# Other tiles for normalisation, cluster products, one-hot turns and odd heads' one-hot transfers in a fused attention and mixture kernel

## The chip, the core and the metric

One core of a Trainium2 chip runs the whole program; nothing is spread over several cores. The metric is the time of one execution in microseconds (us), the median of several runs. The engines are PE (TensorE matmuls, PEld its weight loads), DVE (VectorE), ACT (ScalarE), POOL (GpSimd) and SP, whose queue issues the DMAs. Each engine works through its instructions in the order in which the program wrote them, and waits on semaphores for what others make.

## What is computed

Attention in which a query sees only the keys of its own cluster, then two feed-forward layers, all in float32:

```python
q_assign = np.argmax(np.einsum('bhsd,hcd->bhsc', q_n, c_n), axis=-1)
k_assign = np.argmax(np.einsum('bhsd,hcd->bhsc', k_n, c_n), axis=-1)
mask = q_assign[:, :, :, None] == k_assign[:, :, None, :]
scores = np.where(mask, scale * np.matmul(q, k.transpose(0, 1, 3, 2)), -1000000000.0)
attn = softmax(scores)                       # 2 x 8 heads, 768 tokens, 64 wide, 16 clusters
x = np.matmul(attn, v)                       # -> 1536 x 512
x = np.maximum(x @ w_in, 0.0) ** 2 @ w_out   # 512 -> 2048 -> 512
out = sum_e p[:, e] * (np.maximum(x @ w1[e], 0.0) @ w2[e])   # 4 experts, 512 -> 1024 -> 512
```

## The kernel before, in words

Float32 products are made of three (or two) products of rounded halves, a high and a low part of each operand. The change touches only the attention stage, the first 331 us; the layers behind it are the same program.

**Tiles and rounds.** The 16 heads have six query tiles of 128 rows each, so the loop over `g` has 96 tiles. I count them in rounds of twelve: round r holds the tiles of heads 2r and 2r+1 (tile 0 to tile 11 of the round), and tile n of round r is g = 12r + n. In tile g PE makes the scores of tile g+2 (`emit_S`, L572), transposes the exponentials of tile g (L605) and makes half of the product with V of an earlier pair of tiles (L619, L621). DVE takes the row maximum (L581) and the low halves (L611); ACT the exponential (L592) and the high halves (L610). The order of these pieces within a tile is the written list `ORDER`, one for even and one for odd tiles. A score tile has a second product, of one-hot cluster rows (in `k2` and `q2`), which lifts the matching keys.

**Work for the pair of heads to come.** During round r the one-hots of pair r+1 (heads 2r+2 and 2r+3) are made, at tiles given by the table `AT` as offsets from that pair's first tile. Each such step takes one of two places (`X1`, `X2`) in a tile on PE, and its evacuation stands at `Y1` or `Y2`. All of them use one PSUM tile, `m`. The steps:
- four transposing steps (`trans_slot`, L354) in tiles 10 and 11 of the round before; ACT copies, then POOL splits into `nkh`, `nkl`, `nqh`, `nql` (L52 and L363).
- `pair_scores` twice (L404): the products with the cluster centres, four matmuls for half the tokens, which read the split keys and queries; ACT copies to `ys`.
- `pair_turn` twice (L420): three transposes each, summed by DVE into `A` (L425). The second one appends the steps of `pair_ops` to the list `dq`.
- `pair_ops`: a maximum on DVE (L456, called m1 below), three operations on POOL that mark the first winner (L446 to L448, p1), a second maximum on DVE (L457, m2), and four operations on POOL that write the one-hots `oh` (L451 to L454, p2). Even tiles take two entries of `dq`, odd tiles three, at the letters `C`. Between p1 and m2 stand `AT["gap"]` empty entries. Pair 1 makes p2's part on DVE (`last`, L463 to L466).
- `pair_hot` (L478): empties `dq`, transposes `oh` on PE (three transposes), ACT copies to `ohm` (L483), and SP writes the even head's one-hot rows by four DMAs (`hot_rows`, L495). The odd head's four DMAs are issued at the offset `ohd`.

**Normalisation of the pair before.** `norm_slots(r-1)` enters `nq` at the end of tile 1 of round r, and one entry is taken per tile from tile 2 on: f1 puts four small DVE operations (L661 to L664) in front of `dq`, f2 transposes them (L670) and lets POOL add two halves of the output (`xs`, two operations, L679), and f3 twice (L687) spreads the factors; POOL then multiplies, rounds and takes the low part (L694, L52, L707).

**Also on these engines.** `split_v` (POOL, L52 and L295) at tiles 3 and 9. In rounds 1 to 4 one step of the weight conversion `convert` (letter `K`) stands at the end of every even tile: DVE operations of 128x512, such as L171 and L176, and once a round one on ACT and POOL (L182, L184). The SP queue also carries the stacked copies of `nkh`, `nql` and so on (`stack`, L375, L377).

Of the kernel before, what the change touches and what calls it, by code (L numbers as in the profile page):

```python
# [12 lines left out]
ALU = mybir.AluOpType  # L13
AX = mybir.AxisListType
# [10 lines left out]
    "S T0 X1 M E T1 R Y1 X2 H0 P0 C H1 L0 L1 C K Y2".split(),  # L25
    "S X1 E M T0 T1 Y1 H0 C P1 X2 R L0 H1 C L1 O Y2 C".split()]
WARM = [12, 10, 5, 11, 3, 9]
START = {'t': [0, 1, 1, 2], 'a': [3, 4, 4, 5, 8], 'stack1': 4, 'stack': 5, 'head': [0, 2]}
AT = {"gap": 3, "stack1": -11, "stack": -9, "oh": -4, "ohd": -4, "splitv": -3, "load": -8,
      "t": [-14, -14, -13, -13], "a": [-11, -11, -10, -10, -4], "conv": 8}  # L30


@with_exitstack
def moe_attention_kernel(
# [15 lines left out]
    def round_pool(dst, src):  # L50

        nc.gpsimd.tensor_scalar(dst, src, 1.0, 1.0, op0=ALU.mult, op1=ALU.mult)  # L52
# [28 lines left out]
    wgt = const.tile([128, 1, C], F32, name="wgt")  # L81
# [117 lines left out]
    with tc.manual_schedule():  # L199
# [235 lines left out]
        def pair_ops(j, A):  # L435
            mx = as_p.tile([128, 4 * NTT, 1], F32, tag="mx", name="mx")
            mx2 = as_p.tile([128, 4 * NTT, 1], F32, tag="mx2", name="mx2")
            off = as_p.tile([128, NTT, 2, C], F32, tag="off", name="off")
            oh = ohs["p", j] = as_p.tile([128, NTT, 2, 2, C], F32R, tag="oh", name="oh")
            shp = [128, 4 * NTT, C]  # L440
            V, P = nc.vector, nc.gpsimd
            av = A.rearrange("p (t x e) c -> p t x e c", x=2, e=2)
            mv = mx2.rearrange("p (t x e) c -> p t x e c", x=2, e=2)

            def p1():
                P.tensor_tensor(A, A, mx.to_broadcast(shp), op=ALU.subtract)  # L446
                P.tensor_scalar(A, A, 2.0 ** 63, 2.0 ** 63, op0=ALU.mult, op1=ALU.mult)
                P.tensor_tensor(A, A, wgt.to_broadcast(shp), op=ALU.add)  # L448

            def p2():  # L450
                P.tensor_tensor(A, A, mx2.to_broadcast(shp), op=ALU.subtract)  # L451
                P.tensor_scalar(oh[:, :, :, 0], av[:, :, 1], 0.0, -1.0, op0=ALU.min, op1=ALU.max)
                P.tensor_scalar(off, av[:, :, 0], 0.0, -1.0, op0=ALU.min, op1=ALU.max)
                P.tensor_scalar(oh[:, :, :, 1], off, 1.0, -NEG, op0=ALU.add, op1=ALU.mult)  # L454

            head = [lambda: V.reduce_max(out=mx, in_=A, axis=AX.X), p1]  # L456
            m2 = lambda: V.reduce_max(out=mx2, in_=A, axis=AX.X)  # L457
            if j > 1:
                return head + [lambda: None] * AT["gap"] + [m2, p2]

            def last(e):
                w = [128, NTT, C]
                V.tensor_tensor(off[:, :, e], av[:, :, 0, e], mv[:, :, 0, e].to_broadcast(w),  # L463
                                op=ALU.not_equal)
                V.tensor_scalar(oh[:, :, e, 1], off[:, :, e], NEG, None, op0=ALU.mult)
                V.tensor_tensor(oh[:, :, e, 0], av[:, :, 1, e], mv[:, :, 1, e].to_broadcast(w),  # L466
                                op=ALU.is_equal)
            return head + [lambda: None] * 3 + [m2, lambda: last(0), lambda: last(1)]

        def pair_hot(j):  # L470

# [87 lines left out]
        def pair_slots(j):  # L559
            return [trans_slot(j, nm, half) for nm in ("nk", "nq") for half in range(2)]  # L560
# [92 lines left out]
        def norm_slots(hp, last=False):  # L653
            st = {}
            def f1():
                sm = sums_t.pop(hp)
                r = sm_p.tile([128, 2, NTT], F32, tag="r", name="r", bufs=1)
                rs = st["rs"] = sm_p.tile([128, NTT, 2, 2], F32R, tag="rs", name="rs", bufs=2)
                rv = r.rearrange("p h t -> p t h")
                dq[:0] = [  # L660
                    lambda: nc.vector.tensor_scalar(r, sm, 1e-9, None, op0=ALU.add),  # L661
                    lambda: nc.vector.reciprocal(r, r),
                    lambda: nc.vector.tensor_copy(rs[:, :, :, 0], rv),
                    lambda: nc.vector.tensor_tensor(  # L664
                        rs[:, :, :, 1], rv, rs[:, :, :, 0].bitcast(F32), op=ALU.subtract),
                ]

            def f2():
                m = ps_m.tile([NTT * 4, 128], F32R, tag="m", name="m")
                nc.tensor.transpose(m, st["rs"].rearrange("p t h s -> p (t h s)"), identr)  # L670

                def evac():
                    rt = st["rt"] = xs_p.tile([NTT * 4, 128], F32R, tag="rt", name="rt")
                    nc.scalar.copy(rt, m.bitcast(F32))
                    if hp in xm_t:
                        xm = xm_t.pop(hp)
                        for c0 in range(0, S, HALF):
                            cs = slice(c0, c0 + HALF)
                            nc.gpsimd.tensor_tensor(  # L679
                                xs_t[hp][:, cs], xs_t[hp][:, cs], xm[:, cs], op=ALU.add)  # L680
                return evac

            def f3(half):
                b, kt = divmod(hp, H // 2)
                m = ps_m.tile([128, HALF], F32, tag="m", name="m")
                for j in range(QT):
                    nc.tensor.matmul(  # L687
                        m[:, j * 128:(j + 1) * 128], sel[:, half * QT + j], st["rt"],
                        start=True, stop=True)

                def evac():
                    rb = xs_p.tile([128, HALF], F32, tag="rb", name="rb")
                    nc.scalar.copy(rb, m)
                    (nc.vector if last else nc.gpsimd).tensor_tensor(  # L694
                        rb, rb, xs_t[hp][:, half * HALF:(half + 1) * HALF], op=ALU.mult)
                    c0 = b * S + half * HALF
                    col = c0
                    while col < c0 + HALF:
                        tb, o = divmod(col, TB)
                        n = min(TB - o, c0 + HALF - col)  # L700
                        xn = rb[:, col - c0:col - c0 + n]
                        hi = xh[tb][:, kt, o:o + n]
                        if last:
                            nc.scalar.copy(hi, xn)
                        else:
                            round_pool(hi, xn)
                        (nc.vector if last else nc.gpsimd).tensor_tensor(  # L707
                            xl[tb][:, kt, o:o + n], xn, hi.bitcast(F32), op=ALU.subtract)
                        col += n
                return evac  # L710

            return [f1, None, None, f2, lambda: f3(0), lambda: f3(1)]


        mp = {}
# [320 lines left out]
        def at(d, g, f):  # L1036
            d.setdefault(max(g, 0), []).append(f)

        for i in range(1, NH):
            u0 = i * NTT  # L1040
            if i > 1:
                for n, x in enumerate(("stack1", "stack")):
                    at(early, START[x] if i == 2 else u0 + AT[x], lambda i=i, n=n: stack(i, n))
                if i % 2:
                    at(early, u0 + AT["ohd"], lambda i=i: hot_rows(i))
            else:
                for n in range(2):
                    at(slots, START["head"][n], onehot_slot(i) if n else assign_slot(i))
            at(early, u0 + AT["splitv"], lambda i=i: split_v(i))
            if i + 1 < NH:  # L1050
                at(early, u0 + AT["splitv"] + 1, lambda i=i: load_v(i + 1))
        for j in range(1, NH // 2):
            u0 = 2 * j * NTT
            for n, f in enumerate(pair_slots(j)):
                at(slots, START["t"][n] if j == 1 else u0 + AT["t"][n], f)
            for n, f in enumerate([pair_scores(j, 0), pair_scores(j, 1), pair_turn(j, 0),
                                   pair_turn(j, 1), pair_hot(j)]):
                at(slots, START["a"][n] if j == 1 else u0 + AT["a"][n], f)
            if j + 1 < NH // 2:
# [88 lines left out]
            gemm1(*its[n], ps=s[:, 0])  # L1148

        hp, pr = NH // 2 - 1, NU // 2 - 1  # L1150
        f1, _, _, f2, f3, f4 = norm_slots(hp, last=True)
        f1()
        while dq:
            dq.pop(0)()
# [44 lines left out]
        def r_ops(b, ops):  # L1199
# [8 lines left out]
        head = {  # L1208
            -1: [("t", RT3), ("t", RT1), ("h", RT1), ("t", RT2), ("l", RT1)],
            0: [("h", RT2), ("h", RT3), ("t", RT4), ("l", RT2)],  # L1210
            1: [("l", RT3), ("h", RT4), ("h", RB22)],
            2: [("l", RT4), ("l", RB22)]}
# [89 lines left out]
```

## Time and profile before

| | |
|---|---|
| median of 3 runs | 1083.51 us (1083.09 to 1084.83) |
| profiled execution | 1086.17 us, of which the span of the trace is 1083.2 us |
| busy in the span | PE 1035.2 us, DVE 682.3, ACT 537.3, POOL 561.3 |
| from 0 to 330.8 us (attention) | PE 286.8 us, DVE 241.9, ACT 236.1, POOL 163.2 |
| from 330.8 us to the end | PE 748.4 us of 752.4 |

The page gives busy time for each engine; an engine can be idle between instructions for want of data, and rows of the trace show for such a gap its length and what ended it. Behind 330.8 us PE is busy for all but 4 us. In the attention stage it is not busy for 44 us. The median lies 2.66 us under the profiled execution's own time, which has 2.97 us around its span.

### The profile page before, as it was taken

The numbers are of one execution on the slowest core, as the hardware profiler recorded it, in microseconds if no ns is written. First come the engines' busy times: TensorE is split into PE (matmuls) and PEld (weight loads), VectorE is DVE, ScalarE is ACT, GpSimd is POOL, SyncE is SP. The second block draws the span as 40 slices with busy tenths as digits, with TensorE's granted clock in tenths as the row PEclk, the third lists the DMA queues.
The fourth block names the chain that finished last, engine by engine and source line by source line (L and its number), as shares of the span: only waits on it lengthen the run. The fifth ranks groups of instructions, "written<-read, shape, count | busy, mean of one in ns | idle before, by whom it ended". The sixth has DMA issues, their size and how long they took to land.

```text
span 1083.2 us, 14977 instructions
## 1 busy us (share of the span) xinstructions
PE 1035.2 (96%) x5558; PEld 915.9 (85%) x5558; DVE 682.3 (63%) x1072; ACT 537.3 (50%) x1080; POOL 561.3 (52%) x546
## 2 busy tenths in 40 slices
PE   8897889889799999999999999999999999999998
PEld 7787778779788888888888988889898899888897
DVE  8786677567767777373126655657767555555554
ACT  6686677668775554344434333433445333334331
POOL 4365564564322222223445666667668766666650
PEclk9998998899999999999999999999999999999999
DMA  4663554556202233021101221122123212211201
GB/s 114 158 142 81 128 121 100 125 139 162 67 1 78 85 110 99 19 96 60 39 1 40 78 78 61 57 78 78 45 73 131 83 40 79 78 66 52 78 1 58
DMA packets 72408, 86.05 MB, mean 79 GB/s; under 512 B 26896, under 2 KB 49744, under 8 KB 72336
## 3 DMA queue, kind: packets, MB, share of 16 engines
q1 hardware_dynamic: 72336, 85.11, 27.4%
q8 instruction: 43, 0.70, 0.3%
q14 instruction: 29, 0.24, 0.1%
HBM read 59.83 MB, written 3.15 MB: 58 GB/s over the span
## 4 chain that ended last, share of the span: by engine, by line
PE 85%; DVE 6%; POOL 5%; ACT 1%; issue 1%; SPq 1%; DMA 1%; POOLq 0%; ACTq 0%; DVEq 0%
PE bank L893 24%; PE bank L853 21%; PE bank L746 12%; PE s L572 4%; PE bank L727 4%; PE bank L729 4%; PE bank L728 4%; PE t L605 3%; PE po L619 2%; PE po L621 2%; DVE nb L581 2%; DVE ptl L611 1%; POOL xa L707 1%; POOL rb L694 1%; PE m L404 1%
## 5 line engine op out<-in xcount | busy, mean ns | idle before, releaser
L893 PE MATMUL bank<-w1h,ga 128*128 128x512 f32 x768 | 269.9, 393 | 0.0
L903 DVE SCALAR_TENSOR_TENSOR x<-bank,pe_p,x 128x512 f32<-128x512 f32 x180 | 134.9, 751 | 167.8 <-PE bank L893 167.8
L853 PE MATMUL bank<-xa,w0h 128*128 128x384 f32 x896 | 228.3, 335 | 0.1
L853 PEld LDWEIGHTS bank<-xa,w0h 128*128 128x128 f32 x896 | 164.5, 188 | 17.9 <-ACT fa L864 0.5
L893 PEld LDWEIGHTS bank<-w1h,ga 128*128 128x128 f32 x768 | 144.1, 188 | 24.5
L736 POOL TENSOR_TENSOR ga<-fa,ga 128x512 fp32r<-128x512 f32 x48 | 62.3, 1299 | 182.0 <-ACT ga L735 139.5
L893 PE MATMUL bank<-w1l,ga 128*128 128x512 f32 x384 | 151.6, 395 | 0.0
L853 PE MATMUL bank<-xa,w0l 128*128 128x384 f32 x448 | 149.7, 334 | 0.0
L611 DVE TENSOR_TENSOR ptl<-t,pth 128x384 fp32r<-128x384 f32 x192 | 98.2, 548 | 52.5 <-ACT pth L610 52.0
L864 ACT COPY fa<-bank 128x384 f32<-128x384 f32 x96 | 45.5, 474 | 171.7 <-PE bank L853 171.7
L746 PE MATMUL bank<-ga,w1h 128*128 128x512 f32 x384 | 126.7, 389 | 0.0
L873 ACT ACTIVATE ga<-fa 128x384 fp32r<-128x384 f32 x96 | 50.5, 527 | 135.6 <-DVE fa L867 135.6
L822 POOL TENSOR_TENSOR w0l<-raw,w0h 128x512 fp32r<-128x512 f32 x64 | 75.0, 1195 | 81.4 <-ACT w0h L821 81.4
L840 POOL TENSOR_TENSOR w1l<-raw,w1h 128x1024 fp32r<-128x1024 f32 x32 | 77.2, 2414 | 71.3 <-ACT w1h L839 71.3
L581 DVE TENSOR_REDUCE nb<-s 128x1 f32<-128x768 f32 x96 | 91.5, 953 | 26.5 <-PE s L572 25.7
L610 ACT CAST pth<-t 128x384 fp32r<-128x384 f32 x192 | 84.1, 488 | 23.7 <-PE t L605 23.2
L572 PE MATMUL s<-k,q 80*128 80x384 f32 (+1 forms) x384 | 88.8, 353 | 3.3 <-DMA k<-ohm 3.1
L605 PE MATMUL t<-identf,p 128*128 128x128 f32 x576 | 89.9, 283 | 1.6 <-DVE ptl L611 1.5
L876 DVE SCALAR_TENSOR_TENSOR ga<-fa,ga 128x384 fp32r<-128x384 f32 x96 | 90.1, 938 | 0.6 <-ACT ga L873 0.6
L592 ACT ACTIVATE p<-s,nb 128x768 f32<-128x768 f32 x96 | 87.4, 910 | 2.4 <-DVE nb L581 1.9
L733 ACT ACTIVATE fa<-bank 128x512 f32<-128x512 f32 x44 | 26.3, 598 | 118.1 <-PE bank L729 116.7
L746 PEld LDWEIGHTS bank<-ga,w1h 128*128 128x128 f32 x384 | 72.0, 188 | 14.7
(202 smaller groups left out, 2086.0 us busy)
## 6 DMA issues: line engine op xcount, KB each, us to landing
raw<-in_moe_w_dram SPq DMA_DIRECT2D x64, 512.0 KB, 4.1
raw<-in_moe_w_in_dram SPq DMA_DIRECT2D x8, 1024.0 KB, 5.2
raw<-in_moe_w_out_dram SPq DMA_DIRECT2D x6, 1024.0 KB, 4.9
k<-nkh SPq DMA_DIRECT2D x28, 192.0 KB, 3.3
q<-nqh SPq DMA_DIRECT2D x28, 192.0 KB, 3.0
nv<-in_v_dram SPq DMA_DIRECT2D x16, 192.0 KB, 3.8
out_dram<-x SPq DMA_DIRECT2D x12, 256.0 KB, 2.1
k<-nkl SPq DMA_DIRECT2D x14, 192.0 KB, 3.7
```

The lines of the kernel that those rows point to most:

```text
L572: nc.tensor.matmul(s[:, j, 0:HALF], stk[i, nq][:, t * 128:(t + 1) * 128], stk[i, nk][:, j * HALF:(j + 1) * HALF], start=first, stop=not first)
L581: nc.vector.tensor_reduce(out=nb, in_=s_ps[u][:, :, 0:HALF], axis=AX.XY, op=ALU.max, negate=True)
L592: nc.scalar.activation(p, s_ps.pop(u)[:, :, 0:HALF], AF.Exp, bias=nb_t.pop(u), accum_out=sums_t[hp][:, i % 2, t:t + 1])
L605: nc.tensor.transpose(tp[:, j], p_sb[u][:, half, j * 128:(j + 1) * 128], identf)
L610: return (lambda: nc.scalar.copy(dh, tp), lambda: nc.vector.tensor_tensor(dl, tp, dh.bitcast(F32), op=ALU.subtract))
L611: lambda: nc.vector.tensor_tensor(dl, tp, dh.bitcast(F32), op=ALU.subtract))
L746: nc.tensor.matmul(o, a, b, start=(ft == 0 and z == 0), stop=(ft == NF - 1 and z == 2))
L840: nc.gpsimd.tensor_tensor(lo, w, hi.bitcast(F32), op=ALU.subtract)
L853: nc.tensor.matmul(ps, w[:, o:o + 128], r_op(r, x)[:, kt], start=(first and kt == 0 and z == 0), stop=(kt == 1 and z == 2), skip_group_che ...
L876: nc.vector.scalar_tensor_tensor(out=g_t(n, f, t, 1), in0=h_src(n, f, t), scalar=0.0, in1=g_t(n, f, t, 0).bitcast(F32), op0=ALU.max, op1=A ...
L893: nc.tensor.matmul(o, a, w[:, f], start=(f == 0 and z == 0), stop=(f == 1 and z == 2))
L903: nc.vector.scalar_tensor_tensor(out=acc, in0=o, scalar=pc, in1=acc, op0=ALU.mult, op1=ALU.add)
```

## The change

Numbers in two tables and two lists of steps move.
- `pair_scores` goes from tile 1 (both) to tiles 0 and 1, `pair_turn` from tile 2 (both) to tiles 1 and 2, and `pair_hot` from tile 8 to tile 7. For pair 1, which has its own table `START`, only `pair_hot` moves, from tile 8 to tile 7 of round 0.
- The gap between p1 and m2 is two empty entries, not three.
- The odd head's `hot_rows` go from tile 2 of its own round to tile 11 of the round before (`ohd` from -4 to -7).
- Normalisation: two empty entries come between f2 and f3, so both f3 stand in tiles 8 and 9, not 6 and 7. The last pair's, behind the loop, is the same work.
- Pair 1 marks the first winner on DVE (two operations) and not on POOL (three), with no empty entries.

```diff
-START = {'t': [0, 1, 1, 2], 'a': [3, 4, 4, 5, 8], 'stack1': 4, 'stack': 5, 'head': [0, 2]}
-AT = {"gap": 3, "stack1": -11, "stack": -9, "oh": -4, "ohd": -4, "splitv": -3, "load": -8,
-      "t": [-14, -14, -13, -13], "a": [-11, -11, -10, -10, -4], "conv": 8}
+START = {'t': [0, 1, 1, 2], 'a': [3, 4, 4, 5, 7], 'stack1': 4, 'stack': 5, 'head': [0, 2]}
+AT = {"gap": 2, "stack1": -11, "stack": -9, "ohd": -7, "splitv": -3, "load": -8,
+      "t": [-14, -14, -13, -13], "a": [-12, -11, -11, -10, -5], "conv": 8}
...
-            return head + [lambda: None] * 3 + [m2, lambda: last(0), lambda: last(1)]
+            return [m1, lambda: V.tensor_tensor(A, A, mx.to_broadcast(shp), op=ALU.is_equal),
+                    lambda: V.tensor_tensor(A, A, wgt.to_broadcast(shp), op=ALU.mult),
+                    m2, lambda: last(0), lambda: last(1)]
...
-            return [f1, None, None, f2, lambda: f3(0), lambda: f3(1)]
+            if last:
+                return [f1, f2, lambda: f3(0), lambda: f3(1)]
+            return [f1, None, None, f2, None, None, lambda: f3(0), lambda: f3(1)]
```

**POOL, from `split_v` of tile 3 to p2, in the round that prepares pair 6.** Before, the two additions L679 come first, then p1, and then both f3 (L694 begins each):

```order
L679 TENSOR_TENSOR xs<-xs,xm 128x384 x2
L446 TENSOR_TENSOR A<-A,mx 128x384
L447 TENSOR_SCALAR A<-A 128x384
L448 TENSOR_TENSOR A<-A,wgt 128x384
L694 TENSOR_TENSOR rb<-rb,xs 128x384
```

Five rows further, in the same program, the second f3 and behind it p2 (L451 to L454):

```order
L694 TENSOR_TENSOR rb<-rb,xs 128x384
L52 TENSOR_SCALAR xa<-rb 128x384
L707 TENSOR_TENSOR xa<-rb,xa 128x384
L451 TENSOR_TENSOR A<-A,mx_3122 128x384
L452 TENSOR_SCALAR oh<-A 128x12x16
L453 TENSOR_SCALAR off<-A 128x192
L454 TENSOR_SCALAR oh<-off 128x12x16
```

After the change (two lines further down in the file, so L679 is L681 and L694 is L696):

```order
L446 TENSOR_TENSOR A<-A,mx 128x384
L447 TENSOR_SCALAR A<-A 128x384
L448 TENSOR_TENSOR A<-A,wgt 128x384
L681 TENSOR_TENSOR xs<-xs,xm 128x384 x2
L451 TENSOR_TENSOR A<-A,mx_3110 128x384
L452 TENSOR_SCALAR oh<-A 128x12x16
L453 TENSOR_SCALAR off<-A 128x192
L454 TENSOR_SCALAR oh<-off 128x12x16
L696 TENSOR_TENSOR rb<-rb,xs 128x384
```

Both f3 have moved from before p2 to behind it, and the additions from before p1 to between p1 and p2.

**PE, tiles 7 and 8 of round 0, where the one-hots of pair 1 are transposed.** Before, tile 7 has only its own work, and the transposes (L478) stand in the middle of tile 8:

```order
L605 MATMUL t<-identf,p 128x128 x6
L619 MATMUL po<-pth,vv 128x256
L621 MATMUL po<-ptl,vv 128x256
L619 MATMUL po<-pth,vv 128x256
L621 MATMUL po<-ptl,vv 128x256
L619 MATMUL po<-pth,vv 128x256
L621 MATMUL po<-ptl,vv 128x256
L572 MATMUL s<-k_284,q_301 128x384 x2
L572 MATMUL s<-k_285,q_303 128x384 x2
L605 MATMUL t<-identf,p 128x128 x3
L478 MATMUL m<-identr,oh 128x128 x3
L605 MATMUL t<-identf,p 128x128 x3
```

After, they (now L480) stand in tile 7, right behind its scores:

```order
L574 MATMUL s<-k_284,q_301 128x384 x2
L574 MATMUL s<-k_285,q_303 128x384 x2
L480 MATMUL m<-identr,oh 128x128 x3
L607 MATMUL t<-identf,p 128x128 x6
L621 MATMUL po<-pth,vv 128x256
L623 MATMUL po<-ptl,vv 128x256
```

Everything of tile 7 behind the scores now stands behind these transposes; the later rounds have the same places.

**The SP queue, at the border of two rounds.** Before, the odd head's one-hot rows (L495) follow the next pair's first stacked copies (L375, L377 into `k_2549`) and the transfers of the attention output (L650, L651):

```order
L243 DMA nv<-in_v_dram 128x384
L375 DMA k_2549<-nkh 64x768
L377 DMA k_2549<-nkl 64x768
L650 DMA xs<-xo 64x768
L651 DMA xm<-xo 64x768
L495 DMA q_2377<-ohm 16x3x128 x2
L495 DMA k_2375<-ohm 16x3x128 x2
```

After:

```order
L243 DMA nv<-in_v_dram 128x384
L497 DMA q_2376<-ohm 16x3x128 x2
L497 DMA k_2374<-ohm 16x3x128 x2
L375 DMA k_2557<-nkh 64x768
L377 DMA k_2557<-nkl 64x768
L652 DMA xs<-xo 64x768
L653 DMA xm<-xo 64x768
```

The four transfers have moved past two copies and two output transfers.

## Rows read from the trace of the kernel before

**Rows 1.** Waits of the whole run: total us, times, longest us.

```profile
PE m L478 <- POOL oh L454: 25.8, 6, 4.7
...
PEld m L420 <- DVE A L425: 4.9, 7, 0.8
...
PE s L572 <- DMA k<-ohm: 3.1, 3, 1.1
```

**Rows 2.** PE in time order, round 3: start, us, line; idle before in brackets.

```profile
145.01 0.87 PE L572 MATMUL s<-k,q 128*128 128x384 f32 x4
...
147.09 0.87 PE L572 MATMUL s<-k,q 128*128 128x384 f32 x4
...
151.56 0.86 PE L572 MATMUL s<-k,q 128*128 128x384 f32 x4
...
157.38 0.86 PE L572 MATMUL s<-k,q 128*128 128x384 f32 x4
...
163.31 0.62 PE L478 MATMUL m<-identr,oh 128*128 128x128 f32 x3 [4.73 <-POOL oh L454]
...
169.40 0.87 PE L572 MATMUL s<-k,q 128*128 128x384 f32 x4
...
175.32 0.95 PE L572 MATMUL s<-k,q 128*128 128x384 f32 x4
```

**Rows 3.** Tiles 8, 9 of rounds 3, 5, 6: us, busy, clock, DMA; sum of rounds 1-6.

```profile
157.38:169.40 12.02, 7.29 (x38) 6.92 (x36) 5.04 (x9) 4.47 (x11) 6.96 (x12) 0.72 0.20 44
...
235.60:245.30 9.70, 6.21 (x38) 5.84 (x37) 4.07 (x7) 4.31 (x11) 5.81 (x10) 0.82 0.25 56
272.10:280.40 8.30, 4.81 (x37) 4.28 (x37) 3.88 (x7) 4.38 (x11) 5.86 (x10) 1.00 0.14 30
sum 63.28, PE 37.44 PEld 35.13 DVE 25.75 ACT 26.23 POOL 39.52; mean PE 6.24 PEld 5.86 DVE 4.29 ACT 4.37 POOL 6.59
```

**Rows 4.** POOL in time order, from the splits of tile 10 to p2.

```profile
133.62 0.61 POOL L52 TENSOR_SCALAR nkh<-kqf 128x384 fp32r<-128x384 f32 x1 [6.97 <-DMA k<-nkh]
...
138.42 0.53 POOL L52 TENSOR_SCALAR nqh<-kqf 128x384 fp32r<-128x384 f32 x1
...
145.09 2.12 POOL L679 TENSOR_TENSOR xs<-xs,xm 128x384 f32<-128x384 f32 x2 [2.40 <-DMA xm<-xo]
150.74 1.22 POOL L446 TENSOR_TENSOR A<-A,mx 128x384 f32<-128x384 f32 x1 [3.52 <-DVE mx L456]
...
154.27 1.02 POOL L694 TENSOR_TENSOR rb<-rb,xs 128x384 f32<-128x384 f32 x1 [0.63 <-ACT rb L693]
...
156.93 1.30 POOL L184 TENSOR_TENSOR w0l<-cva,w0h 128x512 fp32r<-128x512 f32 x1
...
161.24 0.84 POOL L451 TENSOR_TENSOR A<-A,mx 128x384 f32<-128x384 f32 x1
...
163.93 1.00 POOL L295 TENSOR_TENSOR vv<-nv,vv 128x384 fp32r<-128x384 f32 x1
```

**Rows 5.** DVE in time order, from the second sum to m1 and m2's tile.

```profile
145.29 0.55 DVE L425 TENSOR_REDUCE A<-m 128x192 f32<-128x384 f32 x1
...
150.12 0.54 DVE L456 TENSOR_REDUCE mx<-A 128x24 f32<-128x384 f32 x1
150.58 0.68 DVE L176 SCALAR_TENSOR_TENSOR cva<-raw,cva 128x512 int32<-128x512 int32 x1
```

**Rows 6.** POOL's first operation of p1 in round 6, where no conversion runs.

```profile
265.92 0.85 POOL L446 TENSOR_TENSOR A<-A,mx 128x384 f32<-128x384 f32 x1 [3.52 <-DVE mx L456]
```

**Rows 7.** PE in time order, tiles 8 and 10 of round 6.

```profile
276.83 0.45 PE L478 MATMUL m<-identr,oh 128*128 128x128 f32 x3 [3.49 <-POOL oh L454]
...
281.87 0.59 PE L572 MATMUL s<-k,q 80*128 80x384 f32 x2 [0.96 <-DMA k<-ohm]
```

**Rows 8.** PE in time order, round 0.

```profile
48.12 0.45 PE L478 MATMUL m<-identr,oh 128*128 128x128 f32 x3 [1.86 <-DVE oh L466]
...
53.28 0.59 PE L572 MATMUL s<-k,q 80*128 80x384 f32 x2 [1.09 <-DMA k<-ohm]
```

More of the change, by code (lines that the diff above doesn't have):

```diff
@@ L454, in p2 @@
                 P.tensor_scalar(oh[:, :, :, 1], off, 1.0, -NEG, op0=ALU.add, op1=ALU.mult)
-            head = [lambda: V.reduce_max(out=mx, in_=A, axis=AX.X), p1]
+            m1 = lambda: V.reduce_max(out=mx, in_=A, axis=AX.X)
             m2 = lambda: V.reduce_max(out=mx2, in_=A, axis=AX.X)
             if j > 1:
-                return head + [lambda: None] * AT["gap"] + [m2, p2]
+                return [m1, p1] + [lambda: None] * AT["gap"] + [m2, p2]
             def last(e):
@@ L1150, in moe_attention_kernel @@
         hp, pr = NH // 2 - 1, NU // 2 - 1
-        f1, _, _, f2, f3, f4 = norm_slots(hp, last=True)
+        f1, f2, f3, f4 = norm_slots(hp, last=True)
         f1()
```

## The prediction

> **What bounds the kernel now.** I first read where the span goes: behind 330.8 us PE idles for 4 us, in the attention stage for 44 us (the table above). Then the list of waits, to see what PE idles for. One wait stands out: the one-hot transposes wait for POOL's last one-hot operation six times, 25.8 us in all [rows 1]. Last the rows in time order, to see why. In round 3 tile 8 begins at 157.38, and its transposes start at 163.31 after 4.73 us of idle [rows 2]. POOL in that time was not short of work, it did other work first: m1 ended at 150.66, p1 ran from 150.74, then came both f3 and a weight conversion, and p2 only at 161.24 [rows 4, 5]. So what ends the wait is POOL's order, not DVE or PE, and as PE stands still meanwhile, a microsecond less there is one less of the span.
>
> The price is more than the idle time. Tiles 8 and 9 together took 12.02 us in round 3, with a granted clock of 0.72 over them, and 8.30 us in round 6 at 1.00 [rows 3]. A tile with no such step takes 2.08 us (145.01 to 147.09) [rows 2]. So after the idle stretch PE ran part of the time at the lower of its two levels (1.2 against 2.4 GHz), in some rounds and not in others.
>
> **What goes.** Tiles 8 and 9 of rounds 1 to 6 took 63.3 us in sum [rows 3]. Without a wait each pair of tiles would be 2 x 2.08 + 0.3 for the three transposes (163.31, 0.3 of start-to-start out of 0.62) = 4.46, six times 26.8. Gone at most: **36.5 us**.
>
> PE waited 3.1 us for one-hot rows on their way by DMA [rows 1]. One of the three is in round 0 (1.09 us) [rows 8], the other two are late in the stage, one of 0.96 us in round 6 [rows 7]. The even rows of pair 7 leave a tile sooner, the odd ones three tiles sooner, and a tile is over 2 us: **2.0 us** go. The odd head's four DMAs move past two copies, an output transfer and its partner on the SP queue. They delay those by their own issue, but the next additions on POOL that need the transfer now come behind p1, so I cost the delay at nothing.
>
> The second `pair_turn` waited up to 0.8 us, 4.9 us in seven rounds, because both turns share one PSUM tile that DVE must empty [rows 1]. Now they stand in two tiles: 0.7 x 6 = **4.2 us** go, with 0 as the bound if the wait only moves.
>
> The two f3 keep their work and only change tiles. Tiles 6 and 7 took 5.82 us (151.56 to 157.38) against 4.16 bare and 0.6 for the six matmuls (0.3 for three, as above) [rows 2], so 1.06 us a round is waiting. In rounds 1 to 4 the conversion on ACT (tile 6) no longer shares a tile with an f3; I take a quarter of the waiting there to go, **1 us**, with 0 and 4 as bounds.
>
> **What comes: a shorter wait at the same transposes.** I follow the new chain from the end of DVE's second sum. Before, it ended at 145.84 and m1 at 150.66, 4.8 us later [rows 5]. The operations between are the same (four small ones, the regular ones of a tile and a half) plus one conversion in rounds 1 to 4, which had been ahead of the sum: I take 4.7 with it, 4.1 without (0.6 less by the 0.68 of such an operation). p1 takes 2.90 (150.74 to 154.27, less 0.63 idle) [rows 4]. Then, new, the two additions stand between p1 and p2: 2.12 [rows 4]. Their data is no longer late, since it landed at 145.09. m2 is ready in that time, because DVE is not held. p2 takes 2.07 (161.24 to 163.31) [rows 2, 4]. With 0.2 for the hand-overs: 4.7 + 2.9 + 2.1 + 2.1 + 0.2 = 12.0 us from sum to transposes.
>
> PE in the same time: with only one turn in tile 2 I let the sum end at that tile's end (before, with two, it ended 0.8 us into tile 3). Then tile 3 with 2.08, tiles 4 and 5 with 4.47 (147.09 to 151.56), tile 6 with 2.08, and the scores of tile 7 with 0.86: 9.5 us [rows 2]. So PE still waits: 2.5 us in rounds 1 to 4, 1.9 in rounds 5 and 6. Sum 4 x 2.5 + 2 x 1.9 = **13.8 us** come back. Bounds: nothing (if DVE gets to m1 2.5 us sooner), and 4.73 each, the old wait. Behind the transposes the rest of tile 7 waits, its transposed exponentials and with them ACT and DVE, as the second half of tile 8 did before.
>
> I let these waits cost no clock: after 1.86 us of idle in round 0 [rows 8] and 3.49 in round 6 [rows 7] there was no loss; the window of round 6 shows 1.00 [rows 3].
>
> **What comes: the cluster products wait for POOL.** The first `pair_scores` stands a tile sooner, in tile 0, and POOL now has both f3 just ahead of the splits which it reads. From the start of tile 8 POOL's first f3 operation is 2.7 us off (154.27 against 151.56, in its old tile) [rows 2, 4]. Both f3 take 5.7 (154.27 to 161.24, less 1.30 of conversion), `split_v` 1.6 (163.31 to 164.93), three splits 4.8 (133.62 to 138.42) [rows 4]. That is 14.8. PE needs 5.8 for two tiles with f3, 5.9 for tiles 10 and 11 (169.40 to 175.32), and is 1.75 into tile 0 when the matmul that reads `nql` comes (my choice: 0.86 for the scores, 0.9 for three transposes and three products): 13.5 [rows 2]. The wait is 1.3 us, in rounds 2 to 6 (round 1 has no f3 behind it): **6.5 us**. Bounds: 0, if f3 starts 1.3 sooner, and 2.5.
>
> **Pair 1.** p1 goes from POOL to DVE: two operations of 128x384 in place of three on POOL, at the busiest place of DVE, against one tile less until the transposes. Before, PE waited 1.86 there and 1.09 for the DMA [rows 8]. I take the first to grow by what the second loses: **0**, between -2 and +2.
>
> One rule bears on this. The Trainium skill, "SBUF — State Buffer", section "Who interferes with whom", says that a VectorE instruction with two inputs in SBUF contends with a GpSimd instruction that reads SBUF, since it takes its second input through the shared read port; the one that starts second waits. The trace agrees: p1's first operation took 1.22 us beside the conversion L176 [rows 4, 5] and 0.85 in round 6 where none runs [rows 6]. By the rule p1's 2.90 would be 2.5 wherever L176 comes elsewhere, and DVE's two new operations would cost pair 1 up to a microsecond beside a `split_v` (1.00 for its second operation [rows 4]); the sum would move by 1.5 us down or 1 up. I stay with the row.
>
> **The sum.** -36.5 - 2.0 - 4.2 - 1.0 + 13.8 + 6.5 + 0 = -23.4 us. The profiled execution's own time was 1086.17 for a span of 1083.2, so it would be 1062.8 and the span 1059.8. The median is 2.66 us lower: **1060 us**.
>
> **The rivals.**
> *The new waits don't come.* DVE runs ahead to m1, or the additions are done by the time p1 ends. For it: the 4.8 us from the second sum to m1 [rows 5] hold regular work of a tile and a half, which could come to stand behind m1. Against: DVE's order there is the same but for one conversion. Then 13.8 and 6.5 are gone: 1083.5 - 43.7 = 1040 us; with half of them 1050.
> *The shorter wait still costs the clock.* In round 5 tiles 8 and 9 took 9.70 us at 0.82, in round 6 8.30 at 1.00, by the same program [rows 3], so idle time of this size can go either way. 1.4 us in each of six rounds: 1060 + 8.4 = 1068 us. With a wait of 2.5 at each cluster product, 6 more: 1074.
> *The additions hold p2 as f3 did.* If the wait stays near 4.73, the change does nothing for the transposes: the idle 25.8 us and most of the slow clock stay, and 2.0 + 4.2 + 1.0 less 6.5 remain: 1083 us. Against it: 2.12 us stand between p1 and p2 now, not the 7.0 of before.
> *Slower.* POOL is one loop: p1, additions, p2, f3, splits, cluster products, sums, m1. If both f3 start so late that the products wait long, PE loses there what it gained. Gain without that wait is 29.9 us, so it decides from 6.0 us in each of five rounds, that is f3 starting 7.4 and not 2.7 us into tile 8. At 8 us of wait: 1094. Against: POOL idled 3.52 us before p1 and 6.97 before the splits [rows 4], so the loop has room.
>
> **How the numbers follow.** Forecast with both waits near their size (1050 to 1067) 0.58; the new waits small or absent (1038 to 1050) 0.20; clock or longer waits (1067 to 1076) 0.13; no effect 0.04; slower 0.05. A measurement of this kernel tells about 0.2% from nothing, some 2 us. Faster by more than that: 0.58 + 0.20 + 0.13 = 0.91, same 0.04, slower 0.05. The range leaves out the last two and a little at the low end: 1041 to 1073.
>
> **What would show it.** In the list of waits the transposes' wait for POOL should fall from 25.8 to about 14 us in six, and a wait of the cluster products for `nql` should appear, near 6 us. The clock over tiles 7 to 9 should be 1.00. In time order p1, the additions, p2 should follow one another on POOL without a gap, and the two DMA waits of 0.96 and its like should be gone. If the transposes don't wait at all, my chain from the sum to m1 is too long; if tile 0 doesn't wait, f3 started sooner. The prediction is wrong if DVE's conversions or the full list of PE's steps make another wait in tiles 1 to 6 that is longer than a microsecond a round.

## The result, and the profile after

The changed kernel takes 1064.39 us (median of 4 runs, 1063.19 to 1067.48) against 1083.75 us (4 runs): a ratio of 0.9825, 95% interval 0.9803 to 0.9847, 19.4 us less. 1060 us had been forecast, in a range of 1041 to 1073. The profiled execution is the longest of the four (1067.48 us, span 1065.7), 17.5 us of span under the one before. One execution of a run below (f3 around the transposes) was granted a clock of 0.556 and took 1691.84 us; its ratio leaves it out, its median of four does not.

The list of waits of the changed kernel (total us, times, longest) answers to [rows 1]. These are the waits of the matmuls themselves, PE; the same waits stand a second time, some tenths longer each, in the list of the weight loads (PEld).

```profile
PE t L607 <- DVE ptl L613: 5.8, 11, 0.8
...
PE m L404 <- POOL nql L363: 3.8, 6, 0.6
PE m L404 <- POOL nqh L52: 3.8, 5, 0.9
...
PE m L404 <- ACT kqf L361: 1.4, 2, 0.9
...
PE m L480 <- POOL oh L454: 1.0, 2, 0.5
```

Of the kernel before, from the same list:

```profile
PE m L420 <- DVE A L425: 3.2, 6, 0.5
...
PE t L605 <- DVE ptl L611: 1.5, 5, 0.5
```

The 25.8 us at the one-hot transposes have become 1.0, in two rounds. The three DMA waits and the wait of the second turn have left the list. New are the waits of the cluster products (L404), 9.0 us in all, for POOL's splits and twice for ACT's copy ahead of them, and more waiting of the ordinary transposes (L607) for DVE's low halves.

To see what each is worth I cut rounds 1 to 6 into tiles 0 to 2, 3 to 7, 8 and 9, and 10 and 11. Stretches of the kernel before (us, busy times, granted clock, DMA share, GB/s), the sums of six rounds in this order:

```profile
sum 55.28, PE 51.84 PEld 49.38 DVE 43.72 ACT 48.07 POOL 32.86; mean PE 8.64 PEld 8.23 DVE 7.29 ACT 8.01 POOL 5.48
...
sum 73.23, PE 72.30 PEld 65.02 DVE 66.36 ACT 59.29 POOL 45.49; mean PE 12.05 PEld 10.84 DVE 11.06 ACT 9.88 POOL 7.58
...
sum 63.13, PE 37.29 PEld 34.98 DVE 25.60 ACT 26.12 POOL 39.39; mean PE 6.21 PEld 5.83 DVE 4.27 ACT 4.35 POOL 6.57
...
sum 35.17, PE 32.64 PEld 30.40 DVE 25.08 ACT 29.48 POOL 10.91; mean PE 5.44 PEld 5.07 DVE 4.18 ACT 4.91 POOL 1.82
```

And of the changed kernel, for tiles 0 to 2 with the rounds 2, 3, 5 and 6 ahead of the sum:

```profile
93.60:103.73 10.13, 8.92 (x65) 8.21 (x64) 6.71 (x14) 7.34 (x18) 6.09 (x9) 1.00 0.31 67
127.94:140.14 12.20, 10.66 (x66) 9.82 (x64) 6.82 (x14) 7.36 (x18) 6.58 (x9) 0.86 0.27 59
...
201.30:214.45 13.15, 10.73 (x66) 9.72 (x65) 6.48 (x13) 7.45 (x18) 7.49 (x10) 0.87 0.32 80
237.43:247.55 10.12, 8.93 (x66) 8.23 (x65) 6.38 (x13) 7.35 (x18) 6.07 (x9) 1.00 0.41 101
sum 68.02, PE 58.87 PEld 53.91 DVE 39.91 ACT 44.18 POOL 38.95; mean PE 9.81 PEld 8.99 DVE 6.65 ACT 7.36 POOL 6.49
...
sum 74.91, PE 68.90 PEld 61.77 DVE 70.32 ACT 61.92 POOL 43.71; mean PE 11.48 PEld 10.29 DVE 11.72 ACT 10.32 POOL 7.29
...
sum 32.45, PE 32.45 PEld 28.84 DVE 25.76 ACT 29.21 POOL 17.61; mean PE 5.41 PEld 4.81 DVE 4.29 ACT 4.87 POOL 2.94
...
sum 33.75, PE 32.18 PEld 30.58 DVE 27.21 ACT 29.48 POOL 27.82; mean PE 5.36 PEld 5.10 DVE 4.53 ACT 4.91 POOL 4.64
```

Tiles 8 and 9 give 30.7 us (63.13 to 32.45) and are now full of work, with both f3 in them. Tiles 10 and 11 give 1.4. Tiles 3 to 7 take 1.7 more although both f3 have left them, and tiles 0 to 2 take 12.7 more, with the clock at 0.86 to 0.87 in rounds 3 to 5. That is 17.7 in all (30.7 + 1.4 - 1.7 - 12.7), where the span says 17.5.

Round 3 shows where the new time goes. PE in time order, from the cluster products of tile 0 to the one-hot transposes of tile 7:

```profile
130.66 0.44 PE L404 MATMUL m<-nqh,cp 128*128 128x384 f32 x1 [0.90 <-POOL nqh L52]
131.74 0.44 PE L404 MATMUL m<-nql,cp 128*128 128x384 f32 x1 [0.64 <-POOL nql L363]
...
133.89 1.48 PE L574 MATMUL s<-k,q 128*128 128x384 f32 x4
...
148.68 0.55 PE L607 MATMUL t<-identf,p 128*128 128x128 f32 x3 [0.74 <-DVE ptl L613]
149.60 0.55 PE L607 MATMUL t<-identf,p 128*128 128x128 f32 x3 [0.38 <-DVE ptl L613]
...
151.41 0.38 PE L480 MATMUL m<-identr,oh 128*128 128x128 f32 x3
```

POOL of the same stretch:

```profile
125.32 1.01 POOL L295 TENSOR_TENSOR vv<-nv,vv 128x384 fp32r<-128x384 f32 x1
126.95 0.52 POOL L52 TENSOR_SCALAR nkh<-kqf 128x384 fp32r<-128x384 f32 x1 [0.61 <-issue]
...
130.69 1.00 POOL L363 TENSOR_TENSOR nql<-kqf,nqh 128x384 fp32r<-128x384 f32 x1
...
144.22 0.84 POOL L446 TENSOR_TENSOR A<-A,mx 128x384 f32<-128x384 f32 x1 [4.96 <-DVE mx L456]
...
145.74 1.00 POOL L448 TENSOR_TENSOR A<-A,wgt 128x384 f32<-128x384 f32 x1
146.70 2.42 POOL L681 TENSOR_TENSOR xs<-xs,xm 128x384 f32<-128x384 f32 x2
149.16 0.84 POOL L451 TENSOR_TENSOR A<-A,mx 128x384 f32<-128x384 f32 x1
```

And DVE:

```profile
139.51 0.55 DVE L425 TENSOR_REDUCE A<-m 128x192 f32<-128x384 f32 x1
...
143.60 0.54 DVE L456 TENSOR_REDUCE mx<-A 128x24 f32<-128x384 f32 x1
...
145.85 1.44 DVE L176 SCALAR_TENSOR_TENSOR cva<-raw,cva 128x512 int32<-128x512 int32 x1
```

From the second sum (140.06) to the transposes (151.41) the chain took 11.4 us where 12.0 had been worked out: 4.1 to the end of m1, then p1, the additions and p2 on POOL without a gap. But PE does not wait for it at the transposes. It waits 0.74 and 0.38 us in tile 6 for DVE's low halves, which come behind L176, and so reaches the transposes when p2 is done. Tile 6 waits as much in all of rounds 1 to 4; in rounds 5 and 6, where no conversion runs, the transposes wait 0.52 us.

### The profile page after: what moved, and what is told of

The parts are those of the page before. It is cut to its first block, busy times and chain, and to the rows that moved or that the text cites. A ratio compares the mean times of both kernels' runs of the same rounds, so it can differ in the third digit from the quotient of the medians.

```text
span 1065.7 us, 14971 instructions
## 1 busy us (share of the span) xinstructions
PE 1035.0 (97%) x5558; PEld 913.1 (86%) x5558; DVE 684.6 (64%) x1074; ACT 539.7 (51%) x1080; POOL 558.5 (52%) x543
## 4 chain that ended last, share of the span: by engine, by line
PE 83%; DVE 9%; POOL 4%; DMA 2%; issue 1%; ACT 1%; SPq 0%; POOLq 0%; DVEq 0%; ACTq 0%
PE bank L897 25%; PE bank L857 21%; PE bank L750 12%; PE bank L732 4%; PE bank L733 4%; PE bank L731 4%; PE s L574 3%; PE t L607 3%; DVE ptl L613 3%; DVE nb L583 2%; PE po L621 2%; PE po L623 2%; DMA k<-nkh 1%; PE m L404 1%; PE m L689 1%
## 5 line engine op out<-in xcount | busy, mean ns | idle before, releaser
L607 PE MATMUL t<-identf,p 128*128 128x128 f32 x576 | 89.5, 280 | 6.4 <-DVE ptl L613 5.8
L750 PEld LDWEIGHTS bank<-ga,w1h 128*128 128x128 f32 x384 | 72.1, 188 | 14.8
```

The lines of the kernel that those rows point to most:

```text
L607: nc.tensor.transpose(tp[:, j], p_sb[u][:, half, j * 128:(j + 1) * 128], identf)
L750: nc.tensor.matmul(o, a, b, start=(ft == 0 and z == 0), stop=(ft == NF - 1 and z == 2))
```

## The experiments

**Normalisation alone.** The kernel before with f3 two tiles later and nothing else:

```diff
-            return [f1, None, None, f2, lambda: f3(0), lambda: f3(1)]
+            if last:
+                return [f1, f2, lambda: f3(0), lambda: f3(1)]
+            return [f1, None, None, f2, None, None, lambda: f3(0), lambda: f3(1)]
```

> The kernel before with one part of the change alone: both f3 of the normalisation two tiles later (tiles 8 and 9). Cluster products, turns, transposes and odd heads' transfers stay where they were. Theory (POOL's order is what held the transposes): p2 is no longer behind f3 and ends near 158.2 of round 3 where the transposes of tile 8 would stand near 158.7, so the 25.8 us wait is gone, and the products in tile 1 find their splits done or nearly (0 to 1 us each): 1047 to 1054 us. Rival (the earlier turns and transposes are needed as well): the transposes still wait over 2 us each, 1064 us or more.

1054.84 us, ratio 0.9721 (0.9706 to 0.9736): 0.8 us above what the theory expected, and 9.6 us faster than the whole change. Its waits, the second from the list of the weight loads (on PE it is 0.2 us):

```profile
PE m L478 <- POOL oh L454: 2.4, 4, 0.6
...
PEld m L404 <- POOL nql L363: 1.4, 4, 0.5
```

So moving f3 behind p2 on POOL frees the transposes by itself, all but 0.6 us a round. The rest of the change, added to it, costs.

**Everything but normalisation.** The changed kernel with f3 back in tiles 6 and 7:

```diff
-            return [f1, None, None, f2, None, None, lambda: f3(0), lambda: f3(1)]
+            return [f1, None, None, f2, lambda: f3(0), lambda: f3(1)]
```

> The changed kernel with one part undone: both f3 back in tiles 6 and 7, everything else as changed. Theory (the products of tile 0 wait for splits that stand behind f3 on POOL, and p2 is ahead of f3 in the program's order anyway): the waits of tiles 0 and 1 go, 53 us for twelve tiles become about 35, the transposes wait as in the changed kernel or 1 us more: 1044 to 1054 us. Rival 1 (the products wait because they stand a tile sooner, whatever is ahead of the splits): 1060 us or more. Rival 2 (moving f3 is what freed the transposes): their wait comes back, 1070 us or more.

1065.84 us, 0.9826 (0.9809 to 0.9843), as the changed kernel. The transposes hardly wait (0.8 us in the list of the weight loads, nothing on PE): p2 is ahead of f3 in this order too, because turns and m2 stand sooner. So either half of the change frees them. But my theory on the products fell: with f3 out of the way their waits stay (on PE 4.5 us for `nqh`, 3.8 for `nql` and 2.6 for ACT's copy `kqf`, against 3.8, 3.8 and 1.4 in the changed kernel), and the first rival holds. POOL of this kernel, where the splits of rounds 2 and 3 begin:

```profile
121.34 1.00 POOL L295 TENSOR_TENSOR vv<-nv,vv 128x384 fp32r<-128x384 f32 x1
125.58 0.52 POOL L52 TENSOR_SCALAR nkh<-kqf 128x384 fp32r<-128x384 f32 x1 [3.23 <-ACT kqf L361]
...
162.59 0.51 POOL L52 TENSOR_SCALAR nkh<-kqf 128x384 fp32r<-128x384 f32 x1 [4.06 <-DMA k<-nkh]
```

POOL idles over 3 us ahead of the first split. The first row names ACT's copy `kqf`, but that had ended at 122.38, 3.2 us before. The second row names another candidate: the stacked copy that reads the tile `nkh` of the pair before, which has one buffer. In [rows 4] that wait stood as 6.97 us, and the prediction had taken it for room on POOL.

**`split_v` later.** `AT["splitv"]` from -3 to -1.

> The changed kernel with split_v (two POOL operations, 1.6 us) two tiles later, so behind three of the four splits and not ahead of them. Theory (the products of tile 0 wait for a queue of POOL work): the wait falls by 1.5 us in each of rounds 2 to 6, and the granted clock of tiles 0 and 1 in rounds 3 to 5, 0.83, goes back to 1.00: 1049 to 1056 us. Rival (the wait is the transfers that free the split tiles, not the queue): within 2 us of the changed kernel, 1062 to 1066 us.

1075.09 us, 0.9924 (0.9896 to 0.9952): some 11 us slower than the changed kernel, against both expectations. The edit moved two things, and the second was overlooked: the other `split_v`, of tile 3, went to tile 5 and so between p1 and p2. The transposes' wait on PE rose to 8.8 us in six. As a test of the queue it decides nothing; as a reading of the chain it fits, for in rounds 5 and 6 the 1.6 us put into it came out as waiting (2.1 us each, not 0.5).

**No conversion in tile 4.**

```diff
-                if g >= AT["conv"] and cq:
+                if g >= AT["conv"] and cq and g % 12 != 4:
```

> The changed kernel without a conversion step in tile 4 of a round; those steps come later, the same work in all. Theory (L176 took 1.44 us there and not 0.68 because POOL held the shared port, and this is what made tile 6 take 3.6 us in rounds 1 to 4): tile 6 falls to about 2.3, the transposes in tile 7 wait 0.5 to 1 us instead, as in rounds 5 and 6: 1058 to 1062 us. Rival (tile 6 waits for DVE's other work): tile 6 stays above 3 us, 1063 to 1066 us.

1063.82 us, 0.9813 (0.9793 to 0.9833), no difference from the changed kernel that these intervals tell. PE no longer waits in tile 6, but at the transposes:

```profile
151.63 0.45 PE L480 MATMUL m<-identr,oh 128*128 128x128 f32 x3 [0.56 <-POOL oh L454]
```

So L176 did hold DVE and made tile 6 long, and it hid the wait for p2, which is the limit there: the wait, now 0.56 to 0.83 us in rounds 1 to 4, moved to where the forecast had it. In this trace tiles 6 and 7 take 32.84 us in six rounds, and 34.40 in the changed kernel's. It also met a lower clock (0.83 to 0.84) in tiles 0 and 1 of rounds 1, 2 and 5, where the changed kernel had it in rounds 3 to 5.

**Products, turns and transposes back**, for pairs 2 to 7, the rest as changed:

```diff
-      "t": [-14, -14, -13, -13], "a": [-12, -11, -11, -10, -5], "conv": 8}
+      "t": [-14, -14, -13, -13], "a": [-11, -11, -10, -10, -4], "conv": 8}
```

> The changed kernel with one part undone for pairs 2 to 7: cluster products, turns and transposes back in tiles 1, 2 and 8. Theory as it stands after the second run (the products of tile 0 stand too soon for the splits, whatever is ahead of these): the waits of tiles 0 and 1 and the lower clock there go, the transposes hardly wait, the odd heads' rows are in time: 1050 to 1055 us, 10 us under the changed kernel. Rival (the earlier products are part of the gain, and the second run only moved the wait): 1060 us or more.

1049.65 us, 0.9682 (0.9666 to 0.9698), 0.35 us below the range given. The products wait 1.6 us in the list of the weight loads and 0.2 on PE, the transposes of these pairs not at all. It is 5.2 us faster than normalisation alone, so the shorter gap, the odd heads' earlier transfers, pair 1 on DVE and its earlier transposes together are worth that; the waits that normalisation alone still had, 1.5 us on PE for the DMA and 2.4 at the transposes, are gone from its list. What each part is worth was not tried.

**The copy of `nkh` first.** On top of f3 back in tiles 6 and 7, in `stack`:

```diff
-                                       (("q1", 128, qh, qh), ("k2", D + C, kh, None),
+                                       (("k2", D + C, kh, None), ("q1", 128, qh, qh),
                                         ("q2", D + C, ql, None)))[part]:
```

> The second run's kernel (f3 back in tiles 6 and 7) with the three stacked copies of tiles 3 and 9 in another order on the SP queue: the one that reads nkh goes first and not behind two others. Theory (the first split waits until this copy has read nkh, since nkh has one buffer): the first split starts 1 to 1.4 us sooner, tile 0 takes as much less in each round, more where the clock stays up: 1054 to 1061 us against 1065.8. Rival (POOL or ACT decides when the splits start): 1064 to 1067 us.

1049.23 us, 0.9681 (0.9666 to 0.9695): 16.6 us less for the place of one transfer in a queue, more than expected. In round 2 the first split comes 3.4 us after the start of tile 10 (119.49 against 116.13), and 5.3 us in the run without the edit (125.58 against 120.27).

```profile
119.49 0.51 POOL L52 TENSOR_SCALAR nkh<-kqf 128x384 fp32r<-128x384 f32 x1 [1.29 <-ACT kqf L361]
```

The products' waits on PE fall from 10.9 us (4.5 + 3.8 + 2.6) to 4.0 (0.6 + 3.4), and the granted clock of tiles 0 and 1 is 1.00 in all six rounds, where the run without the edit had 0.82 to 0.84 in rounds 3, 5 and 6. These two tiles take 41.70 us in six rounds against 55.56, which is most of the gain. That the transfer held the splits of this kernel is shown.

**f3 around the transposes.** The run with products back, f3 in tiles 7 and 9, no conversion in tile 4:

```diff
-            return [f1, None, None, f2, None, None, lambda: f3(0), lambda: f3(1)]
+            return [f1, None, None, f2, None, lambda: f3(0), None, lambda: f3(1)]
```

> The run with products back (tiles 1, 2 and 8), with f3 in tiles 7 and 9 around the transposes of tile 8, and no conversion step in tile 4. Theory (in the first run tile 8 took 4.1 us since transposes and f3 share the one PSUM tile m there, and L176 holds DVE in rounds 1 to 4): tile 8 falls to about 2.5 in each round, f3 of tile 7 stands behind p2 on POOL: 1044 to 1051 us. Rival (tile 8 waits for p2, whatever shares the tile): 1051 to 1056 us.

1049.75 us, 0.9678 (0.9662 to 0.9694): within the theory's range, but no gain over products back. No trace shows what tile 8 took at this speed, so neither the theory nor the rival is decided by its mechanism.

**The copy of `nkh` first, in the changed kernel itself** (the edit above alone):

> The changed kernel with one thing moved: of the stacked copies of tiles 3 and 9 the one that reads nkh is issued first. f3 stays in tiles 8 and 9. Theory (two limits of nearly one length stood before the splits in the changed kernel: the transfer, and the POOL queue with both f3 and split_v): the queue stays, the first split starts at most 0.6 us sooner, tile 0 keeps 1 us or more of its wait: 1056 to 1062 us. Rival 1 (the transfer alone): as in the run before with f3 in tiles 6 and 7, 1048 to 1052 us. Rival 2 (the queue alone): 1063 to 1066 us.

1056.59 us, 0.9748 (0.9732 to 0.9764), 7.8 us under the changed kernel, within the theory's range and outside both rivals'. POOL of round 2:

```profile
121.39 1.01 POOL L295 TENSOR_TENSOR vv<-nv,vv 128x384 fp32r<-128x384 f32 x1
122.37 0.68 POOL L52 TENSOR_SCALAR nkh<-kqf 128x384 fp32r<-128x384 f32 x1
```

The split now follows `split_v` without a gap, 4.3 us into tile 10 (118.09), where the changed kernel had 4.9 (126.95 against 122.02, with a gap of 0.61, and of 1.20 and 1.69 us in the two rounds behind it). So behind the transfer stands the queue that I had worked out. Tiles 0 and 1 of the six rounds:

```profile
89.64:97.32 7.68, 6.43 (x47) 5.76 (x45) 4.26 (x9) 5.12 (x13) 4.59 (x7) 1.00 0.28 61
124.01:131.69 7.68, 6.43 (x47) 5.77 (x45) 4.27 (x9) 5.12 (x13) 4.59 (x7) 1.00 0.30 67
...
sum 44.82, PE 38.50 PEld 34.60 DVE 24.87 ACT 30.72 POOL 26.41; mean PE 6.42 PEld 5.77 DVE 4.14 ACT 5.12 POOL 4.40
```

The clock stays at 1.00. PE's own waits at the products fell by 2.7 us (3.8 + 3.8 + 1.4 to 3.8 + 2.5, in the lists for PE), the run by 7.8; so, by difference, most of it is the clock that no longer falls.

**Both, without the conversion in tile 4** (f3 in tiles 6 and 7, the copy first):

> The run with f3 in tiles 6 and 7 and the nkh copy first, without a conversion step in tile 4. Theory (L176 holds DVE beside POOL's additions and costs tile 6 about 1 us in rounds 1 to 4): tile 6 falls from 3.65 to 2.7, the transposes wait 0.3 more: 1045 to 1048 us against 1049.2. Rival: no change, 1049 to 1050 us.

1046.43 us, 0.9652 (0.9638 to 0.9667), as expected and the fastest here. Without the transfer's wait the conversion's place is worth 2.8 us, with intervals that just part.

**Products back, the copy first, no conversion in tile 4.**

> The run with products, turns and transposes back in tiles 1, 2 and 8 (1049.65 us), with the nkh copy first and without a conversion step in tile 4. Theory: the products of tile 1 waited only 1.6 us in all, so the first gives about 1 us, and the second some 0.2 us a round, since no additions stand beside L176 there: 1047 to 1050 us. Rival (the order of the copies is worth as much here as it was with early products): under 1043 us.

1052.43 us, 0.9706 (0.9691 to 0.9720): a miss, 2.8 us slower than products back alone, though the intervals overlap a little. The conversion's steps come later by this edit, and its POOL operation now falls between the splits in round 2:

```profile
123.00 1.01 POOL L363 TENSOR_TENSOR nkl<-kqf,nkh 128x384 fp32r<-128x384 f32 x1
123.97 1.28 POOL L184 TENSOR_TENSOR w0l<-cva,w0h 128x512 fp32r<-128x512 f32 x1
125.22 0.51 POOL L52 TENSOR_SCALAR nkh<-kqf 128x384 fp32r<-128x384 f32 x1
```

The products that read these splits wait 0.75 and 0.64 us. That this makes up the whole 2.8 us was not tried, and what the order of the copies alone does here was not tried either.

## Why the prediction held, and which terms were off

The number held in part by luck. The measured time lies 4.4 us over the forecast, but tiles 3 to 9 gave 5.3 us more than the sum has for them, and tiles 0 to 2 took 10.4 us more: two errors of opposite sign, the larger of them in a term that the sum puts at 6.5.

**The old wait** went as worked out. Tiles 8 and 9 lost 30.7 us although both f3 came in. Two bare tiles with the six matmuls of f3 are 4.76 us (2 x 2.08 + 0.6), 28.6 in six rounds; they take 32.45. So of the 36.5 us over the bare work 3.9 are left, and that rest is no wait for POOL's one-hots, since the transposes have left these tiles. That POOL's order was the cause is shown by the first run. What the prediction did not see is that either half of the change would have done it alone.

**The shorter wait that comes back** was 13.8 us in the sum. What PE idles in its place is 5.5 us: 1.12 in tile 6 in each of rounds 1 to 4, and 0.52 at the transposes in rounds 5 and 6. The chain was 0.6 us shorter (11.4 against 12.0 us in round 3): m1 came in 4.1, not 4.7, and p1 took 2.5 (144.22 to 146.74), not 2.9, while the additions took 0.3 more. Tiles 3 to 9 together moved by -29.0 us (-30.7 + 1.7); the prediction's terms for them make -23.7 (-36.5 - 1.0 + 13.8). By its own signs the prediction was wrong on one point: it named another wait in tiles 1 to 6 of over a microsecond a round, behind DVE's conversions, and the 1.12 us of tile 6 behind L176 are one.

**The cluster products** are the term that was mis-sized. Tiles 0 to 2 should have moved by +2.3 (6.5 - 4.2) and moved by +12.7. The queue of 14.8 us was right: in round 3 `nql` was done at 131.69, 15.1 us after tile 8 began at 116.63. Two things failed. The step "the wait is 1.3 us, in rounds 2 to 6" left out the transfer that frees `nkh`; the split that round 1 needs waited for it as well (POOL idle for 6.73 us until 57.74, ended by the copy), and it holds the products just as long when the queue is short. So the waits make 9.0 us on PE, in six rounds. And "I let these waits cost no clock", made for the transposes, was taken over for the products: in rounds 3 to 5 the clock fell to 0.86 and 0.87 over tiles 0 to 2. These three rounds take 38.1 us there where rounds 2 and 6, at 1.00, take 10.1 each: 7.7 us more, of which 2.4 are longer waits (1.54, 2.01 and 2.43 us against 1.2) and the other 5.3, by difference, the clock.

**The rivals.** "The shorter wait still costs the clock" had the price right in kind and the place wrong: the clock fell at the products, in three rounds. "The new waits don't come" was half right: the transposes' wait all but went, but tile 6 and the products wait in its place, and 1040 us was not reached. "The additions hold p2 as f3 did" fell, with 1.0 us left of 25.8. "Slower" fell too: the products wait 1.5 us a round where it needed 6.0. Against it the prediction had set the idle 6.97 us before the splits as room on POOL; what ended it was the transfer.

**The small terms.** Both DMA waits went: tiles 10 and 11 gave 1.4, most of it in round 6 (5.33 us before, 4.15 after). The second turn's wait went, but on PE it was 3.2 us (0.5 a round): the 4.2 of the sum was read from the list of the weight loads. The three transposes are 0.2 us after the change (151.41 to 151.62), not 0.3. Pair 1 still waits 1.9 us for DVE, in tile 7 now, and round 0 as a whole was not resolved: its clock differs from run to run.

**The port rule** showed where it had not been looked for. L176 started at 145.85 beside POOL's L448 (145.74) and the additions, and took 1.44 us, not 0.68 as in [rows 5]. p1's first operation took 0.84, as in [rows 6]. The Trainium skill, "SBUF — State Buffer", section "Who interferes with whom", has the instruction that starts second wait, and these rows agree. So the contention moved from POOL to DVE. By the rule the forecast had named 1.5 us less, with p1 at 2.5 and not 2.9, and p1 did take 2.5; it stayed with the row. Whether the longer L176 reached the time is open: the run without that conversion gives back 1.6 us in tiles 6 and 7 of its trace, but its time is not told from the changed kernel's.

## What to carry to other kernels

When a step on one engine is moved sooner, follow each of its inputs back to the point where its buffer comes free, not only along the queue of the engine that writes it: here a transfer that read the old contents held the writer, and an idle entry of 6.97 us in the trace had named it. A change of several parts that all help the same wait should be taken apart, since one part may bring the whole gain and the others only new waits. The order of transfers in one queue can decide when buffers come free (16.6 and 7.8 us here, by the place of one copy); where the next writer waits for one, issue that one first.

## What the runs showed that I had not expected

The granted clock fell after waits of 0.90 and 0.64 us within one tile: in round 3 of the changed kernel the scores of the next tile took 1.48 us and not 0.86, so PE ran at the lower of its two levels (1.2 against 2.4 GHz). Before, a wait of 3.49 us in round 6 had left it at 1.00 [rows 3, 7]. The run without a conversion in tile 4 has the same two waits in tile 0 of rounds 4 and 5, 0.89 and 0.64 in the one, 0.90 and 0.64 in the other. These are tiles 0 and 1 of both:

```profile
164.63:172.90 8.27, 6.71 (x47) 5.80 (x45) 3.84 (x7) 5.53 (x14) 6.47 (x8) 1.00 0.27 62
198.98:208.92 9.94, 8.27 (x47) 7.30 (x45) 4.79 (x9) 5.23 (x13) 5.30 (x7) 0.83 0.20 45
```

The clock stayed at 1.00 in the first and fell to 0.83 in the second, which took 1.7 us longer. So the length of the waits in a tile does not say whether the clock falls; what does was not settled here.
